# Two transformer layers on one core: GpSimd yields to VectorE's two-input operations, and the bias b2 moves to VectorE

## The chip, the cores and the metric

The kernel runs on one core of one Trainium2 chip. The metric is the device time of one execution in microseconds (us), as a median over runs. The core has five engines that each run their own instruction list in order and meet only at semaphores: TensorE (PE; PEld is its weight load), ScalarE (ACT), VectorE (DVE), GpSimd (POOL) and SyncE (SP), which issues the DMAs. Operands live in SBUF; TensorE writes to the eight banks of PSUM, 128 x 512 float32 each.

## The reference

Two layers with the same weights, each an attention block and a dense block, on 2048 tokens of width 512; 32 heads of width 16; the dense block is 1792 wide. All tensors are bf16.

```python
def _A_ref(x, wqkv, wo):
    qkv = (x @ wqkv).reshape(B, S, 3, H, Dh) ...
    scores = jnp.einsum("bhqd,bhkd->bhqk", q, k) * (Dh ** -0.5)
    p = _softmax(scores, axis=-1)
    o = jnp.einsum("bhqk,bhkd->bhqd", p, v)
    return o ... @ wo

def _B_ref(x, w1, b1, w2, b2):
    h = _gelu(jnp.einsum("bsd,df->bsf", x, w1) + b1)
    return jnp.einsum("bsf,fd->bsd", h, w2) + b2

x = x + _A_ref(_layernorm(x), A_wqkv, A_wo)
x = x + _B_ref(_layernorm(x), B_w1, B_b1, B_w2, B_b2)
# and the same two lines once more
```

## The kernel before

**Tiles and stages.** Tokens go in 16 tiles of 128, and queries in segments of 512 (the last segment of the second layer is split in two of 256). A layer is a long row of *passes*: a pass is one segment and four heads (for the two half segments, eight heads): 32 passes a layer, some of them cut in two by key range. A pass holds 64 *cells*: the scores of 128 keys against 512 query columns in one PSUM bank, their exponential, and the product of that with V, which adds up in PSUM bank 6. There are 4096 cells in all.

**Two ways for a cell.** Most cells go to ScalarE: `exps` (L1828) takes two or three banks in one exp instruction (L1846) and writes bf16 to a `pt` buffer. About 30% go by VectorE and GpSimd: `dfirst` (L1566) turns the scores into a 16-bit integer whose bits are an approximate power of two (L1568, tile `du`, or one of the lent tiles `kt` and `v`), and `dchain` (L1639) makes three shifted copies by two GpSimd integer additions (L1658 for one copy, L1662 for the two others), each of which is multiplied with a V scaled to it, so that the errors of the approximation average out. Those scaled copies of V, `vc`, are made by VectorE in `vcopies` (L1330).

**Around the passes.** VectorE also masks Q for each pass (`qpad`, L1347, tile `qp`), closes each pass (`norm`, L935: transpose out of bank 6, reciprocal, two-input product `ott` at L977, transpose to `otn`), adds the output projection to x (`wo`, L1014), normalises tiles (`ln`, L755, many small operations on `varr`, `rstd`, `ra`, `rb`, `nmr`, then `xln` at L802), adds b1 (L1123) and adds the dense block's result to x (`ytile`, L1174). The normalised tile goes through a DMA transpose to `xf` (L806, on SP's queue). TensorE does projections, dense layers (all recorded at L628, in groups of four 32-column matmuls side by side), scores (L1399) and P.V (L1912, with L1920 for the unused column groups).

**The order.** None of the engine lists is written by hand. Each piece of work is a generator that yields operations `_Op(engine, cost, ...)`; `_Sched` keeps a planned clock for each engine, takes from all threads the operation that can start first by that clock (ties by priority, a low number first), and appends it to its engine's list with the semaphore waits that its operands need. So the order on each engine is a result of the planned costs, and any change of a cost moves thousands of instructions. Every 24 us of planned ScalarE time, `tune` (L409) loads another of 15 sets of knobs, named by the list `PICKS` (L111).

**What the plan does about GpSimd and VectorE.** VectorE operations marked `port` (L239: those that write `ott`, `nmr`, `qp`, `vc`, `xln`, `varr`, `rstd`, `ra`, `rb` and a few more, reading first from SBUF) and GpSimd's additions are planned not to overlap. In `_ready` (L338) a GpSimd operation starts after the last `port` operation that began before it, and has an explicit wait for it; a `port` operation that would begin inside a planned GpSimd operation is planned at that operation's end. Priority does not enter there: a GpSimd addition that can start, starts.

**Filler.** Where a planned gap on TensorE is long enough and its density over the last 3.4 us (`WINDOW`) is under `WARM`, `fill` (L387) puts in matmuls whose result nobody reads (L1387).

**b2.** Row 0 of the tile `B2row` holds b2, the other rows are zeroed by GpSimd at the start (L646, L707). In `ytile` (L1148) the first operation of each tile begins with four matmuls of `ONES1` (ones in row 0) and `B2row` (L1167), which start the sum in PSUM; 14 further groups of four add the dense product, and L1174 adds the bank to x.

Of the kernel before, what the change touches and what calls it, by code (L numbers as in the profile page):

```python
# [5 lines left out]
ALU = mybir.AluOpType  # L6
# [8 lines left out]
D = 512  # L15
# [16 lines left out]
XT = 8  # L32
# [34 lines left out]
WTAIL = 2.8  # L67
RUSH = 8
# [42 lines left out]
PICKS = (1, 8, 1, 3, 1, 8, 1, 2, 8, 1, 8, 3, 0, 1, 1, 0, 0, 0, 0, 2, 1, 11, 8, 8,  # L111
         1, 8, 8, 3, 1, 1, 8, 1, 9, 8, 8, 1, 1, 8, 1, 3, 8, 1, 1, 8, 7, 2, 2, 14,
         7, 7, 1, 7, 7, 1, 9, 1, 1, 1, 1, 1)
# [115 lines left out]
class _Op:  # L229
    __slots__ = ("eng", "cost", "fns", "reads", "writes", "sem", "by", "tail", "prio", "mode", "slack", "late", "back", "port", "limit", "after")  # L230

    def __init__(self, eng, cost, fns, reads=(), writes=(), sem=None, by=1, tail=0.0, prio=None, mode="F", slack=None):
        self.eng, self.cost = eng, cost
        self.fns = fns if isinstance(fns, list) else [fns]
        self.reads, self.writes = list(reads), list(writes)
        self.sem, self.by, self.tail, self.prio, self.mode, self.slack = sem, by, tail, prio, mode, slack
        self.limit = 1e9
        self.late, self.after = None, []
        self.port = eng == "dve" and self.writes[:1] != [] and self.writes[0].startswith(("OTT", "NMR", "QP", "VC", "XLN", "PT", "V0", "V1", "VARR", "RSTD", "RA", "RB")) and not self.reads[:1] == [] and not self.reads[0].startswith("B.")  # L239
# [13 lines left out]
OWN = 0.022  # L253
HEAD = 0.14
LATENCY = {"pe": 0.219, "act": 0.21, "dve": 0.139, "pool": 0.153328, "sp": 0.1}
# [4 lines left out]
class _Sched:  # L260
# [77 lines left out]
    def _ready(self, op):  # L338
        t = 0.0
# [16 lines left out]
        return t  # L356

# [260 lines left out]
class _Plan:  # L618
# [12 lines left out]
    def init(self):  # L631
# [14 lines left out]
        yield _Op("pool", 0.3, lambda e: e.memset(T["B2row"][:], 0.0), writes=["B2zero"])  # L646
# [34 lines left out]
    def loads(self):  # L681
# [20 lines left out]
        for t in range(4, 8):  # L702
# [4 lines left out]
        yield _Op("sp", 0.2, lambda e: e.dma_start(T["B2row"][0:1, :], hbm["b2"].rearrange("(o e) -> o e", o=1)),  # L707
                  reads=["B2zero"], writes=["B2row", "B2zero"], sem="db2", by=16, tail=2.0)
# [46 lines left out]
    def ln(self, tiles, dst, dkeys, prio, quick=False, gate=()):  # L755
# [34 lines left out]
        for t in tiles:  # L790
            yield ("spawn", self.ln_tile(c, t, dst, dkeys, quick), prio)

    def ln_tile(self, c, t, dst, dkeys, quick):
# [5 lines left out]
        else:  # L799
# [348 lines left out]
    def ytile(self, l, seg, t):  # L1148
# [9 lines left out]
        for p in range(NFC // 2):  # L1158
# [11 lines left out]
            yield _Op("pe", len(fns) // 4 * MM, fns, reads=[wk, "ONES1", "B2row"] + ["G.%d.%d" % (f, t % 4) for f in (2 * p, 2 * p + 1)],  # L1170
                      writes=["B.%d" % b], prio=MID if p else FPRIO, mode="P")
# [149 lines left out]
    def vcopies(self):  # L1321
        T = self.T
        for l in range(NL):
            for j, kt in enumerate(KD[l]):
# [4 lines left out]
                for i, w in enumerate(VW):  # L1329
                    yield _Op("dve", 0.42, lambda e, j=j, i=i, w=w, src=src: e.tensor_scalar(  # L1330
# [5 lines left out]
    def qpad(self):  # L1336
        T = self.T
        for pi, (l, seg, g, kts, part, final) in enumerate(self.pas):
# [7 lines left out]
            for i, t in enumerate(ts):  # L1346
                yield _Op("dve", 0.15 + 0.262 * w / 512, lambda e, s=s, q=q, i=i, t=t, w=w: e.tensor_scalar(  # L1347
# [167 lines left out]
    def scores(self):  # L1515
        u = 0
        pools = self.s.pools
        while True:
# [24 lines left out]
            ahead = 0.065 + 0.4267 * self.held[1 - sl]  # L1543
# [284 lines left out]
    def exps(self):  # L1828
        T = self.T
        u = 0  # L1830
        while True:
# [14 lines left out]
            yield _Op("act", 0.065 + 0.4267 * n, lambda e, src=src, dst=dst: e.activation(  # L1846
# [178 lines left out]
```

## Time and profile before

Three runs took 1440.49, 1442.47 and 1443.03 us (median 1442.47). The profiled execution took 1441.41 us, of which its span, from the first to the last instruction, is 1439.5.

| | us, or as said | from |
|---|---|---|
| profiled execution / span | 1441.41 / 1439.5 | times, page |
| exps of two banks, `pt` alone | 893, mean 1.059 | ScalarE by form |
| exps of three banks, `pt` alone | 175, mean 1.503 | ScalarE by form |
| du, kt and v copies (L1568) | 1217, mean 0.68 | groups |
| GpSimd additions | 1240 in all, 0.60 and 1.02 for two cells | groups |
| filler matmuls, L1387 without the 13 at the start | 456 | PE by form |
| b2 matmuls | 128, mean 0.387 | PE by form |
| granted TensorE clock | 1.000 | cores |
| busy from 12 to 1411 us, of 1399.0 | PE 1357.2, ACT 1388.8, DVE 1195.7, POOL 1000.4 | windows |
| busy from 1411 us to the end, of 28.5 | PE 25.7, ACT 11.1, DVE 12.5, POOL 1.3 | windows |

A row of the groups reads: line, engine, operation, output<-input with shapes, count | busy us, mean ns of one | idle time of the engine just before such an instruction, and what ended most of it. Busy time counts overlapping instructions of an engine once, so an instruction's mean duration can be longer than the distance from its start to the next one's. A wait row reads: who waited, for whom: us in total, times, longest.

### The profile page before, as it was taken

What the parts mean: (1) busy time and instruction counts of PE and PEld (TensorE: products, weight loads), DVE (VectorE), ACT (ScalarE), POOL (GpSimd) and SP (SyncE); (2) the same over time, 40 slices, a digit from 0 to 9 for tenths busy, and PEclk for the clock granted to TensorE, in tenths of its full rate; (3) what the DMA queues carried; (4) which work ended last, traced back from release to release, by engine and by line L of the source; (5) the groups of instructions that cost most, each with busy time, mean ns of one, the idle gap of its engine ahead of it and who ended that gap; (6) DMA issues with size and microseconds to landing.
All of it is one profiled execution on the core that took longest, in us unless ns stands there. A gap on an engine that the chain in (4) does not pass through costs nothing.

```text
span 1439.5 us, 46034 instructions
## 1 busy us (share of the span) xinstructions
PE 1391.2 (97%) x19654; PEld 421.6 (29%) x19654; DVE 1215.7 (84%) x2266; ACT 1404.3 (98%) x1397; POOL 1006.0 (70%) x1261
## 2 busy tenths in 40 slices
PE   8999999999999999999999999999999999999998
PEld 3222222222222222222222222222222222344345
DVE  7789998978999889997988777999878986899774
ACT  7999999999999999999999999999999999999994
POOL 1177998767787686885757667658777876787670
PEclk9999999999999999999999999999999999999999
DMA  5200001153121531115321161100134115421443
GB/s 162 53 2 1 2 17 30 39 168 91 38 46 31 155 111 39 38 38 148 99 65 43 54 193 53 31 15 18 38 108 143 38 38 157 132 52 33 148 112 90
DMA packets 145047, 103.38 MB, mean 72 GB/s; under 512 B 37069, under 2 KB 143822, under 8 KB 144846
## 3 DMA queue, kind: packets, MB, share of 16 engines
q1 hardware_dynamic: 144846, 100.44, 24.5%
q8 instruction: 158, 2.59, 0.7%
q14 instruction: 43, 0.35, 0.1%
HBM read 88.61 MB, written 4.19 MB: 64 GB/s over the span
## 4 chain that ended last, share of the span: by engine, by line
ACT 47%; PE 36%; DVE 14%; DMA 2%; issue 1%; POOL 1%; SPq 0%; ACTq 0%
ACT pt L1846 36%; PE ps L628 12%; PE ps L1912 12%; PE ps L1399 11%; DVE du L1568 6%; ACT g L1144 3%; ACT v L1846 2%; ACT q L1846 2%; DVE kt L1568 2%; DMA xf<-xln 1%; ACT kt L1846 1%; ACT g L1846 1%; DVE v L1568 1%; DVE stats L762 1%; DVE xln L802 1%
## 5 line engine op out<-in xcount | busy, mean ns | idle before, releaser
L1846 ACT ACTIVATE pt<-ps 128x1024 bf16<-128x1024 f32 (+1 forms) x1069 | 1077.3, 1131 | 6.2 <-PE ps L1399 5.0
L1568 DVE TENSOR_SCALAR du<-ps 128x512 uint16<-128x512 f32 x899 | 597.6, 682 | 118.5 <-PE ps L1399 114.3
L1399 PE MATMUL ps<-qp,kt 32*128 32x512 bf16 x4096 | 535.0, 384 | 16.5 <-ACT pt L1846 9.2
L1662 POOL INT64_ADD du<-du x458 | 468.3, 1024 | 62.8 <-DVE qp L1347 9.4
L1658 POOL INT64_ADD du<-du x458 | 276.5, 605 | 248.1 <-DVE du L1568 194.5
L1912 PE MATMUL ps<-du,vc 128*17 128x512 bf16 (+1 forms) x3000 | 355.1, 359 | 3.5 <-POOL du L1662 1.1
L1399 PEld LDWEIGHTS ps<-qp,kt 32*128 32x128 bf16 x4096 | 137.8, 90 | 560.0 <-issue 175.6
L1912 PE MATMUL ps<-pt,v 128*17 128x512 bf16 (+1 forms) x2564 | 291.0, 360 | 4.4 <-ACT pt L1846 2.1
L1912 PE MATMUL ps<-du,v 128*17 128x512 bf16 (+1 forms) x1000 | 163.9, 360 | 5.7 <-issue 1.5
L628 PE MATMUL ps<-xf,wr 128*32 128x512 bf16 (+1 forms) x2272 | 160.7, 371 | 4.1 <-DMA xf<-xln 3.4
L1568 DVE TENSOR_SCALAR kt<-ps 128x512 uint16<-128x512 f32 x201 | 135.9, 684 | 26.7 <-PE ps L1399 25.2
L1912 PE MATMUL ps<-kt,vc 128*17 128x512 bf16 (+1 forms) x720 | 142.2, 346 | 0.7 <-POOL du L1662 0.4
L1912 PEld LDWEIGHTS ps<-du,vc 128*17 128x17 bf16 x3000 | 94.2, 89 | 81.4 <-issue 36.6
L1662 POOL INT64_ADD kt<-kt x103 | 104.9, 1019 | 12.3 <-DVE qp L1347 1.6
L628 PE MATMUL ps<-wr,g 128*32 128x512 bf16 x1504 | 110.9, 382 | 0.5 <-DMA wr<-in_B_w_dram 0.3
L1912 PEld LDWEIGHTS ps<-pt,v 128*17 128x17 bf16 x2564 | 69.2, 88 | 81.7 <-issue 51.0
L1123 DVE TENSOR_SCALAR g<-ps,hb1t 128x512 bf16<-128x512 f32 (+1 forms) x112 | 79.1, 708 | 13.6 <-PE ps L628 13.5
L1568 DVE TENSOR_SCALAR v<-ps 128x512 uint16<-128x512 f32 x117 | 79.1, 683 | 12.1 <-PE ps L1399 11.6
L1912 PE MATMUL ps<-kt,v 128*17 128x512 bf16 (+1 forms) x359 | 85.1, 358 | 3.0 <-DVE xt L968 1.3
L1658 POOL INT64_ADD kt<-kt x103 | 62.2, 604 | 34.5 <-DVE kt L1568 27.5
L1846 ACT ACTIVATE q<-ps 128x1024 bf16<-128x1024 f32 (+1 forms) x81 | 84.5, 1103 | 0.0
L1912 PE MATMUL ps<-v,vc 128*17 128x512 bf16 (+1 forms) x411 | 82.9, 350 | 0.6 <-DVE xln L802 0.5
(110 smaller groups left out, 1482.8 us busy)
## 6 DMA issues: line engine op xcount, KB each, us to landing
wr<-in_B_w_dram SPq DMA_DIRECT2D x243, 256.0 KB, 3.0
wr<-in_A_wqkv_dram SPq DMA_DIRECT2D x24, 256.0 KB, 2.9
wr<-in_A_wo_dram SPq DMA_DIRECT2D x17, 256.0 KB, 3.0
x<-in_A_x_dram SPq DMA_DIRECT2D x7, 512.0 KB, 4.1
pt<-in_B_w_dram SPq DMA_DIRECT2D x13, 256.0 KB, 3.7
kept<-x SPq DMA_DIRECT2D x4, 512.0 KB, 4.4
x<-kept SPq DMA_DIRECT2D x4, 512.0 KB, 4.0
out_dram<-x SPq DMA_DIRECT2D x16, 128.0 KB, 3.0
```

Source lines behind the costliest of these rows:

```text
L628: return [lambda e, a=a: e.matmul(out[32 * a:32 * a + 32, :], lhsT=lhsT[:, 32 * a:32 * a + 32], rhs=rhs, start=start, stop=stop, tile_posi ...
L762: yield _Op("dve", 0.66, lambda e, t=t: e.bn_stats(T["STATS"][:, t, :], T["X"][:, t % XT, :]), reads=["X.%d" % (t % XT)], writes=["ST.%d" ...
L802: yield _Op("dve", 0.41, lambda e: e.tensor_scalar(xl, T["X"][:, t % XT, :], T["RSTD"][:, t:t + 1], T["NMR"][:, t:t + 1], op0=ALU.mult, op ...
L1123: yield _Op("dve", 0.21 + n / 966, lambda e, fc=fc, pb=pb: e.tensor_scalar(T["G"][:, fc, q], pb, T["HB1T"][:, fc:fc + 1], None, op0=ALU.ad ...
L1144: lambda e, g=g: e.activation(out=g, in_=g, func=ACT.Gelu_apprx_tanh), reads=gk, writes=gk, prio=2)
L1399: return (lambda e: e.matmul(o, lhsT=lhsT, rhs=rhs, start=True, stop=True, tile_position=(32 * a, 0)), ["K%d.%d.%d" % (l, gb, kt // 4), "Q ...
L1568: yield _Op("dve", 0.682, lambda e: e.tensor_scalar(u, self.bank(b), E_SCALE, E_BIAS, op0=ALU.mult, op1=ALU.add), reads=["B.%d" % b], writ ...
L1658: yield _Op("pool", 0.151 + 0.2176 * n, lambda e: e.int64_add(words(1, 1), words(0, 1), SHIFT * ONES), reads=key[0], writes=key[1])
L1662: yield _Op("pool", 0.143 + 0.4352 * n, lambda e: e.int64_add(words(2, 2), words(0, 2), 2 * SHIFT * ONES), reads=key[0] + key[1], writes=k ...
L1846: yield _Op("act", 0.065 + 0.4267 * n, lambda e, src=src, dst=dst: e.activation(out=dst, in_=src, func=ACT.Exp, scale=0.25), reads=["B.%d" ...
L1912: op.fns.append(lambda e, o=o, lhsT=q[0][0][m], rhs=q[0][1][:, n * m:n * m + n], a=a, st=st, sp=sp: e.matmul(o, lhsT=lhsT, rhs=rhs, start= ...
```

## The change

Five edits, all in the planner's program:

1. **GpSimd yields.** A GpSimd operation is not a candidate while some thread's next operation is a `port` operation of priority 1 or lower number whose inputs are planned to be there within 0.6 us (`held_off`). Layer-norm threads have priority 0.2 or 0.3 (those of the first layer's opening 5 and up), `norm` threads 0.1 or 1, `qpad` and `vcopies` 4.
2. **b2 by VectorE.** `B2row` is loaded into all 128 rows by one DMA. As soon as a tile's `xln` is made for the dense block, a thread (priority of the norm plus 1) adds `B2row` to the tile's x in SBUF; `ytile` waits for it before its own sum. The four matmuls go, and the first dense matmul starts the sum in the bank. x is now also a `port` output when it is the b2 sum.
3. **Planned durations.** An exp costs 0.052 us plus 0.4267 a bank (was 0.065), a `qp` copy 0.08 + 0.262 (was 0.15 + 0.262), a `vc` copy 0.31 (was 0.42), and a DMA transpose lands 4.4 us after its issue (was 3.5).
4. **Another `PICKS`.**
5. GpSimd's memset of `B2row` goes.

```diff
+TTAIL = 4.4
-PICKS = (1, 8, 1, 3, 1, 8, 1, 2, 8, 1, 8, 3, 0, 1, 1, 0, 0, 0, 0, 2, 1, 11, 8, 8,
...
+PICKS = (1, 1, 2, 1, 2, 0, 1, 2, 1, 1, 11, 1, 2, 1, 2, 2, 1, 1, 2, 2, 2, 2, 1, 5,
...
-        self.port = eng == "dve" and ... "RSTD", "RA", "RB")) and ...
+        self.port = eng == "dve" and ... "RSTD", "RA", "RB", "X.")) and ...
+HOLDP = 1
+HOLDT = 0.6
         if op.eng == "pool":
+            if HOLDP and self.held_off(max(t, self.clock["pool"])):
+                return None
             t = max(t, self.last(max(t, self.clock["pool"]))[0])
+    def held_off(self, at):
+        for th in self.threads:
+            op = th.op
+            if op is not None and op.port and self._prio(op) <= HOLDP and all(k in self.P.lastw for k in op.reads):
+                t = max([self.end.get(ev, 0.0) - OWN * (ev[0] == "dve") for ev in self.P.deps(op.reads, op.writes)] + [0.0])
+                if t <= at + HOLDT:
+                    return True
+        return False
-        yield _Op("pool", 0.3, lambda e: e.memset(T["B2row"][:], 0.0), writes=["B2zero"])
-        yield _Op("sp", 0.2, lambda e: e.dma_start(T["B2row"][0:1, :], hbm["b2"].rearrange("(o e) -> o e", o=1)),
-                  reads=["B2zero"], writes=["B2row", "B2zero"], sem="db2", by=16, tail=2.0)
+        yield load(T["B2row"][:], hbm["b2"].rearrange("(o e) -> o e", o=1).to_broadcast([128, D]), "db2", ["B2row"], 0.4)
+    def bias(self, t, ph):
+        T = self.T
+        yield _Op("dve", 0.42, lambda e: e.tensor_tensor(out=T["X"][:, t % XT, :], in0=T["X"][:, t % XT, :], in1=T["B2row"][:, :], op=ALU.add),
+                  reads=["X.%d" % (t % XT), "B2row"], writes=["X.%d" % (t % XT)])
+        yield ("give", ("b2", ph // 2, t))
@@ ln_tile, behind xln @@
+        if ph % 2:
+            yield ("spawn", self.bias(t, ph), prio + 1)
-                      reads=["XLN.%d" % x], writes=dkeys(t), sem="dtr%d" % x, by=16, tail=3.5)
+                      reads=["XLN.%d" % x], writes=dkeys(t), sem="dtr%d" % x, by=16, tail=TTAIL)
@@ ytile @@
-            fns = [] if p else self.quads(pb, T["ONES1"][:, :], T["B2row"][:, :], True, False)
+            fns = []
             for j in range(2):
-                fns += self.quads(pb, T["G"][:, 2 * p + j, q], ws[j], False, p == last and j == 1)
+                fns += self.quads(pb, T["G"][:, 2 * p + j, q], ws[j], not (p or j), p == last and j == 1)
+        yield ("need", ("b2", l, t))
@@ vcopies, qpad, scores, exps @@
-                    yield _Op("dve", 0.42, ...
+                    yield _Op("dve", 0.31, ...
-                yield _Op("dve", 0.15 + 0.262 * w / 512, ...
+                yield _Op("dve", 0.08 + 0.262 * w / 512, ...
-            ahead = 0.065 + 0.4267 * self.held[1 - sl]
+            ahead = 0.052 + 0.4267 * self.held[1 - sl]
-            yield _Op("act", 0.065 + 0.4267 * n, ...
+            yield _Op("act", 0.052 + 0.4267 * n, ...
```

What the two planned programs hold, counted in their instruction lists:

| instructions | before | after |
|---|---|---|
| exps of three / two / one bank | 204 / 1133 / 1 | 177 / 1175 / 0 |
| score blocks copied by VectorE (L1568) | 1217 | 1215 |
| GpSimd additions | 1240 | 1232 |
| score matmuls, in so many unbroken runs | 4096, 1333 | 4096, 1356 |
| P.V matmuls with the zero ones beside them | 8984 | 8956 |
| filler matmuls without the 13 at the start | 456 | 320 |
| b2 matmuls / b2 additions on VectorE | 128 / 0 | 0 / 32 |
| explicit waits of GpSimd for VectorE | 710 | 718 |

More of the change, by code (lines that the diff above doesn't have):

```diff
@@ L238, in __init__ @@
         self.late, self.after = None, []
-        self.port = eng == "dve" and self.writes[:1] != [] and self.writes[0].startswith(("OTT", "NMR", "QP", "VC", "XLN", "PT", "V0", "V1", "VARR", "RSTD", "RA", "RB")) and not self.reads[:1] == [] and not self.reads[0].startswith("B.")
+        self.port = eng == "dve" and self.writes[:1] != [] and self.writes[0].startswith(("OTT", "NMR", "QP", "VC", "XLN", "PT", "V0", "V1", "VARR", "RSTD", "RA", "RB", "X.")) and not self.reads[:1] == [] and not self.reads[0].startswith("B.")
 class _Thread:
@@ L1166, in ytile @@
                 wk, ws = "WR.%d" % w, [T["WR"][w][:, 512 * j:512 * j + 512] for j in range(2)]
[L1167 removed]
+            fns = []
             for j in range(2):
[L1169 to L1170 removed]
+                fns += self.quads(pb, T["G"][:, 2 * p + j, q], ws[j], not (p or j), p == last and j == 1)
+            yield _Op("pe", len(fns) // 4 * MM, fns, reads=[wk] + ["G.%d.%d" % (f, t % 4) for f in (2 * p, 2 * p + 1)],
                       writes=["B.%d" % b], prio=MID if p else FPRIO, mode="P")
```

14 lines of the change are left out of this document (7 added, 7 removed).

## The prediction

> **What bounds the kernel now.** I read the page's busy shares and its chain first, then ScalarE by form, then the waits, then the places where ScalarE starts late. The page:
>
> ```profile
> PE 1391.2 (97%) x19654; PEld 421.6 (29%) x19654; DVE 1215.7 (84%) x2266; ACT 1404.3 (98%) x1397; POOL 1006.0 (70%) x1261
> ACT 47%; PE 36%; DVE 14%; DMA 2%; issue 1%; POOL 1%; SPq 0%; ACTq 0%
> ```
>
> ScalarE and TensorE are both full, and the chain hops between them: ScalarE cannot take an exp before TensorE has its scores, TensorE cannot write scores before ScalarE has freed the bank. VectorE and GpSimd have 224 and 433 us to spare. ScalarE by form, and a stretch of its timeline:
>
> ```profile
> L1846 ACT ACTIVATE pt<-ps 128x1024 bf16<-128x1024 f32 x893 | 856.1, 1059 | 5.4 <-PE ps L1399 4.3
> L1846 ACT ACTIVATE pt<-ps 128x1536 bf16<-128x1536 f32 x175 | 251.7, 1503 | 0.8 <-PE ps L1399 0.7
> ...
> 403.42 1.03 ACT L1846 ACTIVATE v<-ps 128x1024 bf16<-128x1024 f32 x1
> 404.32 7.91 ACT L1846 ACTIVATE pt<-ps 128x1024 bf16<-128x1024 f32 x8
> ```
>
> One two-bank exp lasts 1.03 to 1.06 us, but the next starts 0.90 us after it: exps overlap at their ends. Three banks go 1.33 us apart, so an exp costs 0.052 + 0.427 per bank. Summing start-to-start minus this price over the trace from 30 to 1404 us, ScalarE loses 36.1 us: 4 us in jitter under 0.03, 20.8 in 222 delays of 0.03 to 0.25, 11.3 in 24 longer ones. That is all an order can win back between the first and the last exp; 12 us of start and 28.5 of tail stand outside.
>
> **The change part by part**, against the profiled execution's 1441.41 us (span 1439.5 and 1.9 around it; the median of the runs, 1442.47, is 1.06 above it).
>
> *b2 off TensorE.* 32 tiles lose four matmuls each.
>
> ```profile
> 1430.02 0.39 PE L628 MATMUL ps<-b2row,ones 128*32 128x512 bf16 x4
> 1430.23 2.76 PE L628 MATMUL ps<-q,g 128*32 128x512 bf16 x48
> ```
>
> The four run side by side: what follows starts 0.21 us later, so 32 x 0.21 = 6.7 us. Four tiles lie after the last exp (1416.5, 1418.0, 1430.0, 1433.3), where TensorE works without a gap and sets the end: **-0.8**. The other 28 take 5.9 us out of the steady part.
>
> *The other order, on TensorE.* In the built programs' instruction order the 4096 score matmuls stand in 1356 runs instead of 1333. What a run costs:
>
> ```profile
> 1375.19 0.40 PE L1912 MATMUL ps<-du,v 128*17 128x256 bf16 x8
> 1375.41 0.39 PE L1912 MATMUL ps<-du,vc 128*17 128x256 bf16 x8
> 1375.73 0.39 PE L1399 MATMUL ps<-qp,kt 32*128 32x512 bf16 x3
> 1376.06 0.28 PE L1912 MATMUL ps<-v 128*17 128x256 bf16 x1
> ```
>
> Eight P.V matmuls take 0.22 (1375.19 to 1375.41); the score run starts 0.32 after the second eight, 0.10 more than that, and work behind it 0.33 later: 0.43 a run. 23 x 0.43 = +9.9; 28 fewer P.V and zero matmuls, four abreast, -1.5; b2 -5.9: +2.5 net. TensorE has 36% of the chain, so I count **+0.9** (ends: 0 and +2.5). 136 fewer filler matmuls (34 x 0.21 = 7.1 us) I take at nothing, since they are put where TensorE idles; were they in the way, 36% of it, -2.6, would be gained.
>
> *The other order, on ScalarE.* 1215 instead of 1217 score blocks go by VectorE and GpSimd, and 1352 exps instead of 1338: 2 x 0.427 + 14 x 0.052 = **+1.6**, all of it on the busiest engine (ends: +1.6 and, at the 47% share, +0.8).
>
> *GpSimd held back.* What it cures:
>
> ```profile
> L977 DVE TENSOR_TENSOR ott<-xt,rc 128x256 bf16<-128x256 f32 x56 | 36.1, 644 | 1.1
> L802 DVE TENSOR_SCALAR xln<-x,rstd,nmr 128x512 bf16<-128x512 bf16 x60 | 26.2, 469 | 2.9 <-DMA kt<-xln 2.0 <-DMA xf<-xln 0.7
> L780 DVE TENSOR_TENSOR ra<-rstd 128x4 f32<-128x4 f32 x20 | 5.0, 251 | 0.1
> ...
> L977 DVE TENSOR_TENSOR ott<-xt,rc x72: 277/424/1274, 92.0 to 1413.8; 128x256 bf16<-128x256 f32 x56, 128x128 bf16<-128x128 f32 x16
> ```
>
> The same ott lasts 0.42 or up to 1.27 us, as long as a GpSimd addition (1.02) more. By the records, 81 VectorE operations last over 0.12 us longer than the lower quartile of their kind, 33 us together; 62 of them (27 us: ott 13.9, the norm's small ones and xln 13.1) have a priority that the hold covers; the qp copies (5.3) do not. But VectorE has slack, and the price is what ScalarE feels: in the 5 us after those stalls it loses 10.7 us where its mean rate gives 8.1, in the 2 us after, 3.9 for 4.1. So **-1.5**, between 0 and 27 us x 14% of the chain = -3.8. One place:
>
> ```profile
> 523.03 1.04 POOL L1662 INT64_ADD du<-du  x1 [0.30 <-DVE rstd L783]
> 524.12 0.39 PE L1912 MATMUL ps<-du,v 128*17 128x512 bf16 x1 [0.41 <-POOL du L1662]
> ```
>
> The addition waited for the norm, P.V for the addition, and the exp after it came 0.56 late. The additions that are now begun later lie in GpSimd's 433 idle us; if that cover were gone, P.V would wait for them as here.
>
> *b2 added by VectorE.* 32 additions, two bf16 tiles in, one out. No row has it: nearest is xln (one tile in, 0.41 unhindered), then vc (0.29) and x<-x,ps (0.68, one input in PSUM). At 0.41: 13.1 us in VectorE's slack; 14% of that is 1.8, and most waits nowhere since the tile's own sum comes long after: **+0.5** (ends 0 and 0.68 x 32 x 14% = +3.0). The Trainium skill's page "VectorE: DVE Perf Modes" (Side-by-side: where the cycles go for N=2048 bf16) gives a two-input bf16 operation two elements a cycle behind some 158 cycles of start: an estimate of 0.43 us, which would leave the sum as it is. The memset that falls away (0.52 at the start on GpSimd) and the wider b2 load are both before anyone needs b2: nothing, at most the memset's 0.5.
>
> *Transposes planned 0.9 us later.* In the waits and at the worst place:
>
> ```profile
> PE ps L628 <- DMA xf<-xln: 3.4, 4, 1.3
> ...
> 880.88 0.61 PE L628 MATMUL ps<-xf,wr 128*32 128x512 bf16 x8 [1.28 <-DMA xf<-xln]
> 881.87 1.02 ACT L1846 ACTIVATE pt<-ps 128x1024 bf16<-128x1024 f32 x1 [1.08 <-PE ps L1399]
> ```
>
> TensorE's queue holds a projection whose input is not there; the scores stand behind it. Four such waits, and ScalarE starts 0.51, 0.91, 1.21 and 0.16 late behind them. With a later plan other work stands there: **-2.7** (ends 0 and -3.4).
>
> *The rest of the order.* 36.1 - 2.7 - 1.5 = 32 us of lateness remain, decided by where the planner puts each piece. Its new prices are nearer the trace: exp 0.052 + 0.427 a bank (it had 0.065), qp copy 0.342 (clean records 0.341, it had 0.412), vc 0.31 (0.29 clean, it had 0.42). By 36-us slices ScalarE loses 0.4 to 2.4 us, 0.8 in the middle one. Levelled to the middle one, 38 x 0.8 = 30: 6 less, of which the 4.2 above are part; to the best, 0.5: 17 less. Since a new order brings new late places too, I take **-4** (ends +6 and -13).
>
> Sum: -0.8 + 0.9 + 1.6 - 1.5 + 0.5 - 2.7 - 4 = -6.0: 1435.4 profiled, 1436.5 as a median.
>
> **Rivals.** *The order is worth more.* TensorE's fewer fillers mark fewer slack stretches; if all slices lose as little as the best, the rest gives -13 for -4: 1427.5. Against: 76 of the 136 fillers vanish in two of sixteen parts of the score sequence.
> *The stalls were hidden anyway.* ScalarE pays +1.6 and gets only the tail, -0.8, and half of the transposes, -1.4: 1442. For it: lateness after port stalls is no higher than elsewhere. This is also the time if the hold does not do what it says: it orders the plan's clock, and explicit GpSimd waits for VectorE rise only from 710 to 718.
> *The b2 addition collides.* Its priority is above the hold's bound, so GpSimd may have begun: ott's 28 stalls were 0.50 each. At 0.41 + 0.2 mean, it keeps the copies behind it from freeing PSUM banks for the scores. It decides where VectorE has under 0.6 us of slack behind it; at 24 of 32 places that is 14.6 us over a sum without its 0.5: 1450.5. Against: VectorE's copies waited 114 us for scores, so they usually have slack.
> *The clock drops.* Fewer fillers could let TensorE fall under the density that the kernel keeps over 3.4 us. Ten such windows at half speed cost 17 us: 1453. Against: the same rule places the fillers, the granted clock is 1.00 and the longest gap in the steady part 1.46 us. The page "TensorE: Matmul & The Clock Gate" of the Trainium skill (Part 1: The HAM clock gate) has the clock halve after an idle window of that length; no run here shows it.
>
> **How the numbers follow.** The forecast 0.55 (its own range 1430 to 1441), more from the order 0.13, hidden 0.17, colliding addition 0.13, clock 0.02. The likeliest gives **1436.5**. 1424 to 1448 leaves out part of the second, most of the fourth and the fifth, about 0.15. Within 0.2% (2.9 us, about what this measurement tells from no change) is 1439.6 to 1445.4: faster 0.50 + 0.13 + 0.01 = 0.64; same 0.05 + 0.14 = 0.19; slower 0.02 + 0.13 + 0.02 = 0.17.
>
> **What would show it.** ScalarE's lateness between first and last exp near 29 us; no wait of TensorE for xf<-xln over 0.3; ott's mean under 0.50 and the norm's small operations under 0.18; the b2 additions near 0.41; 1352 exps; a tail under 28 us. Wrong if ott falls and ScalarE's lateness stays at 36 (hidden), if rows of scores waiting for VectorE grow behind the b2 additions (colliding), or if score runs wait for GpSimd more than before.

## The result, and the profile after

The changed kernel takes 1449.82 us (median of 5 runs, 1449.70 to 1450.66) against 1443.03 for the kernel before in the same comparison: a ratio of 1.0050, 95% interval 1.0035 to 1.0065. The forecast was 1436.5, and 1449.8 lies above its range too. The profiled execution took 1449.72 us, its span is 1447.9. From the page of the changed kernel, the busy shares and the shares of the chain:

```profile
PE 1388.9 (96%) x19362; PEld 416.8 (29%) x19362; DVE 1233.6 (85%) x2296; ACT 1407.6 (97%) x1411; POOL 1002.4 (69%) x1252
ACT 44%; PE 32%; DVE 22%; POOL 2%; issue 1%; ACTq 0%; POOLq 0%; DVEq 0%
```

ScalarE and TensorE have as much to do as before. What moved is the chain: VectorE's share rises from 14 to 22%, though its busy time rose by only 18 us (1215.7 to 1233.6). ScalarE by form, and two rows of the waits:

```profile
L1867 ACT ACTIVATE pt<-ps 128x1024 bf16<-128x1024 f32 x899 | 863.8, 1081 | 10.9 <-PE ps L1420 9.4
L1867 ACT ACTIVATE pt<-ps 128x1536 bf16<-128x1536 f32 x155 | 225.5, 1521 | 2.9 <-PE ps L1420 2.6
...
PEld ps L1420 <- DVE du L1589: 95.2, 209, 1.0
ACT pt L1867 <- PE ps L1420: 12.0, 32, 1.0
```

The same two waits in the kernel before:

```profile
PEld ps L1399 <- DVE du L1568: 79.0, 188, 0.8
ACT pt L1846 <- PE ps L1399: 5.0, 10, 1.1
```

Score matmuls wait 16 us more for a VectorE copy (L1589, the old L1568) to free their bank, and exps wait 7 us more for scores. Read by the prediction's own measure, ScalarE's start-to-start minus 0.052 + 0.427 a bank, the lateness between first and last exp is 46.2 us, and 37.0 in the kernel before worked out the same way. The exps by that price come to 1.6 us more (two banks and 14 exps more), and together that puts the end of the last exp at 1421.8 instead of 1410.8. The tail behind it is 26.1 us instead of 28.7. So 11.0 lost before the last exp, 2.6 won after it: 8.4, the difference of the spans.

Where the lateness grew: I took, for each of 17 layer-norm chains, the time from its first `varr` to 3 us past its last `xln`. Inside these *norm stretches* lateness rose from 9.7 to 23.1 us; outside them it fell from 27.3 to 23.1. A chain from `varr` to `nmr` takes 5.57 us on average for 8.36 before, and 215 other VectorE instructions stand between `varr` and the last `xln` where there were 362. VectorE's rows by form show the rest:

```profile
L997 DVE TENSOR_TENSOR ott<-xt,rc 128x256 bf16<-128x256 f32 x56 | 33.2, 592 | 0.9
L820 DVE TENSOR_SCALAR xln<-x,rstd,nmr 128x512 bf16<-128x512 bf16 x60 | 27.5, 493 | 0.1
L807 DVE TENSOR_TENSOR x<-x,b2row 128x512 bf16<-128x512 bf16 x32 | 17.6, 563 | 0.0
L795 DVE SCALAR_TENSOR_TENSOR rstd<-rb,rstd 128x2 f32<-128x2 f32 x18 | 6.5, 362 | 0.4 <-DVE rb L793 0.2
L792 DVE TENSOR_TENSOR ra<-rstd 128x4 f32<-128x4 f32 x20 | 4.7, 234 | 0.1
```

The same `rstd` row in the kernel before:

```profile
L783 DVE SCALAR_TENSOR_TENSOR rstd<-rb,rstd 128x2 f32<-128x2 f32 x18 | 3.2, 177 | 0.2
```

The operations for which GpSimd is held back are not free of it. `ott` is a little shorter (644 to 592 ns), `xln` longer (469 to 493), and of the small operations some have grown, this `rstd` to twice its mean (177 to 362), and some have not (`ra` on 128x4, 251 to 234). In all, 105 VectorE operations last over 0.12 us longer than the lower quartile of their kind, 43.7 us together; before it was 81 and 33.2. One place, chosen rows of the timeline (start, duration, engine and instruction; idle time before it in brackets):

```profile
980.74 1.04 POOL L1683 INT64_ADD du<-du  x1 [0.17 <-DVE rstd L795]
981.11 0.69 DVE L792 TENSOR_TENSOR ra<-rstd 128x4 f32<-128x4 f32 x1
981.72 0.68 DVE L1589 TENSOR_SCALAR du<-ps 128x512 uint16<-128x512 f32 x1
982.32 0.14 DVE L793 SCALAR_TENSOR_TENSOR rb<-ra,varr 128x4 f32<-128x4 f32 x1
982.39 0.67 DVE L1589 TENSOR_SCALAR du<-ps 128x512 uint16<-128x512 f32 x1
982.45 0.39 PE L1420 MATMUL ps<-qp,kt 32*128 32x512 bf16 x3 [0.35 <-DVE du L1589]
983.12 0.38 PE L1420 MATMUL ps<-qp,kt 32*128 32x512 bf16 x1 [0.28 <-DVE du L1589]
...
984.28 1.94 ACT L1867 ACTIVATE pt<-ps 128x1024 bf16<-128x1024 f32 x2 [0.37 <-PE ps L1420]
984.57 0.39 PE L1420 MATMUL ps<-qp,kt 32*128 32x512 bf16 x3 [0.33 <-DVE du L1589]
985.03 1.50 DVE L820 TENSOR_SCALAR xln<-x,rstd,nmr 128x512 bf16<-128x512 bf16 x2
987.00 1.02 ACT L1867 ACTIVATE pt<-ps 128x1024 bf16<-128x1024 f32 x1 [0.78 <-PE ps L1420]
```

The addition starts at 980.74 and ends at 981.78. `ra`, four numbers a row, starts inside it and ends at 981.80: 0.69 us for an operation that takes 0.15 when nothing is in its way. The copy behind it frees its bank half a microsecond late, the scores behind the copies wait (0.35, 0.28, 0.33), and ScalarE stands idle for 0.37 and then 0.78 us. The Trainium skill, page "SBUF — State Buffer" (Who interferes with whom), says that VectorE shares one pair of SBUF ports with GpSimd, and that who issues first has it for its whole instruction while the other is blocked; these lines agree, `ra` ends 0.02 us behind the addition.

The 0.78 has a second cause besides. The windows of 3.4 us before and behind 985.40 (busy time of each engine, number of instructions in brackets, then the granted clock of TensorE):

```profile
core 0: us, PE busy (x) PEld busy (x) DVE busy (x) ACT busy (x) POOL busy (x), PEclk, DMA share, GB/s
981.99:985.40 3.41, 2.23 (x26) 0.61 (x26) 3.41 (x9) 3.04 (x4) 2.62 (x4) 1.00 0.01 2
985.40:988.82 3.42, 3.42 (x34) 0.55 (x26) 3.19 (x6) 2.15 (x3) 2.76 (x4) 0.50 0.21 42
```

While the scores waited, TensorE was busy 2.23 of 3.41 us, and for the next 3.4 us its clock was granted at half; there ScalarE lost 1.27 us, for 0.37 in the window before. This place alone, of all the norms in this trace, has that. It is not what makes the kernel slow: two of the five executions ran at a clock of 1.000 and took 1449.70 and 1449.97 us, as long as the others.

What lets that addition start there can be read in the code. While `ra` is a candidate, `held_off` keeps the addition out of the choice. As soon as `ra` has been placed, the addition is a candidate again. Its own start has not moved: it is the later of its inputs and GpSimd's clock, which lies up to 0.6 us *ahead* of `ra`. And `last` looks only at `port` operations that began at or before that start (`LEAN` is 0.0), so the addition gets neither a later start nor a wait. Going through the placed operations, in 84 of the 1232 additions a `port` operation is planned to begin inside the addition, over 0.2 us before its end (the addition itself begins 0.02 to 0.75 us ahead of that operation). In the kernel before this is so in none of the 1240, since such an operation is placed towards the addition's end. The hold thus removes the rule that kept room for the collision, and leaves the collision.

### The profile page after: what moved, and what is told of

Its sections match the earlier page's. It is cut to its first block, busy times and chain, and to the rows that moved or that the text cites. A ratio compares the mean times of both kernels' runs of the same rounds, so it can differ in the third digit from the quotient of the medians.

```text
span 1447.9 us, 45508 instructions
## 1 busy us (share of the span) xinstructions
PE 1388.9 (96%) x19362; PEld 416.8 (29%) x19362; DVE 1233.6 (85%) x2296; ACT 1407.6 (97%) x1411; POOL 1002.4 (69%) x1252
## 4 chain that ended last, share of the span: by engine, by line
ACT 44%; PE 32%; DVE 22%; POOL 2%; issue 1%; ACTq 0%; POOLq 0%; DVEq 0%
ACT pt L1867 31%; PE ps L1420 10%; PE ps L1933 10%; PE ps L642 10%; DVE du L1589 8%; ACT q L1867 3%; ACT v L1867 3%; ACT g L1164 3%; DVE kt L1589 2%; ACT kt L1867 2%; POOL du L1683 1%; DVE xln L820 1%; DVE v L1589 1%; DVE ott L997 1%; DVE stats L774 1%
## 5 line engine op out<-in xcount | busy, mean ns | idle before, releaser
L1867 ACT ACTIVATE pt<-ps 128x1024 bf16<-128x1024 f32 (+1 forms) x1054 | 1060.1, 1146 | 13.8 <-PE ps L1420 12.0
L1589 DVE TENSOR_SCALAR du<-ps 128x512 uint16<-128x512 f32 x896 | 598.7, 683 | 110.5 <-PE ps L1420 105.2
L1420 PE MATMUL ps<-qp,kt 32*128 32x512 bf16 x4096 | 540.1, 384 | 27.3 <-ACT pt L1867 10.0
L1933 PE MATMUL ps<-du,vc 128*17 128x512 bf16 (+1 forms) x2988 | 347.3, 360 | 4.5 <-POOL du L1683 1.2
L1420 PEld LDWEIGHTS ps<-qp,kt 32*128 32x128 bf16 x4096 | 141.6, 91 | 582.9 <-issue 184.3
L1933 PE MATMUL ps<-pt,v 128*17 128x512 bf16 (+1 forms) x2523 | 283.4, 359 | 4.2 <-ACT pt L1867 2.2
L1589 DVE TENSOR_SCALAR kt<-ps 128x512 uint16<-128x512 f32 x201 | 134.9, 682 | 25.8 <-PE ps L1420 25.1
L1933 PE MATMUL ps<-kt,vc 128*17 128x512 bf16 (+1 forms) x723 | 133.8, 345 | 1.4 <-DVE du L1589 0.5
L1933 PEld LDWEIGHTS ps<-du,vc 128*17 128x17 bf16 x2988 | 92.2, 89 | 82.4 <-issue 36.2
L1589 DVE TENSOR_SCALAR v<-ps 128x512 uint16<-128x512 f32 x118 | 79.3, 683 | 14.8 <-PE ps L1420 14.7
L1867 ACT ACTIVATE q<-ps 128x1024 bf16<-128x1024 f32 (+1 forms) x83 | 88.1, 1132 | 0.6 <-PE ps L1420 0.5
L1867 ACT ACTIVATE g<-ps 128x1024 bf16<-128x1024 f32 (+1 forms) x85 | 84.8, 1116 | 0.8 <-PE ps L1420 0.5
```

What stands on the lines that cost most here:

```text
L1420: return (lambda e: e.matmul(o, lhsT=lhsT, rhs=rhs, start=True, stop=True, tile_position=(32 * a, 0)), ["K%d.%d.%d" % (l, gb, kt // 4), "Q ...
L1589: yield _Op("dve", 0.682, lambda e: e.tensor_scalar(u, self.bank(b), E_SCALE, E_BIAS, op0=ALU.mult, op1=ALU.add), reads=["B.%d" % b], writ ...
L1867: yield _Op("act", 0.052 + 0.4267 * n, lambda e, src=src, dst=dst: e.activation(out=dst, in_=src, func=ACT.Exp, scale=0.25), reads=["B.%d" ...
L1933: op.fns.append(lambda e, o=o, lhsT=q[0][0][m], rhs=q[0][1][:, n * m:n * m + n], a=a, st=st, sp=sp: e.matmul(o, lhsT=lhsT, rhs=rhs, start= ...
```

## The experiments

Each run is compared with the kernel before on the same chip. Ratios carry their 95% intervals; where they are turned into time, 0.001 is 1.44 us. "Stalls" and "lateness" are measured as above.

| run | median us | ratio (interval) | stalls: number, us | lateness us |
|---|---|---|---|---|
| changed kernel | 1449.82 | 1.0050 (1.0035 to 1.0065) | 105, 43.7 | 46.2 |
| e1, hold off | 1452.05 | 1.0077 (1.0060 to 1.0093) | 92, 37.8 | 32.7 |
| e2, hold alone | 1471.48 | 1.0210 (1.0195 to 1.0225) | 96, 42.4 | 64.1 |
| e3, b2 sum on 2 columns | 1446.85 | 1.0042 (1.0027 to 1.0057) | 96, 40.8 | 42.9 |
| e4, all additions short | 1425.79 | 0.9893 (0.9878 to 0.9908) | 5, 0.9 | 20.9 |
| e5, forgotten waits added | 1449.47 | 1.0054 (1.0039 to 1.0069) | 88, 36.2 | 46.2 |
| e6, the same on e2 | 1461.94 | 1.0139 (1.0124 to 1.0154) | 63, 26.7 | 51.2 |
| e7, before, all additions short | 1432.70 | 0.9936 (0.9920 to 0.9953) | 4, 0.8 | 27.4 |
| e8, P.V does not wait for GpSimd | 1447.49 | 1.0040 (1.0025 to 1.0055) | 110, 46.2 | 42.9 |
| e9, 84 held additions short | 1427.83 | 0.9897 (0.9877 to 0.9916) | 39, 11.0 | 23.0 |
| e10, 84 others short | 1447.71 | 1.0039 (1.0027 to 1.0051) | 88, 38.9 | 43.3 |
| e11, hold made good, choices anew | 1439.09 | 0.9981 (0.9972 to 0.9990) | 61, 23.0 | 29.7 |
| e12, hold off, choices anew | 1438.89 | 0.9975 (0.9966 to 0.9985) | 87, 33.9 | 25.9 |
| e13, as e11, other choices | 1439.40 | 0.9989 (0.9979 to 0.9998) | 59, 20.4 | 27.9 |
| e14, as e12, other choices | 1443.12 | 1.0010 (1.0001 to 1.0019) | 88, 35.2 | 27.1 |
| e15, 65 held additions at norms short | 1428.60 | 0.9907 (0.9894 to 0.9921) | 62, 20.7 | 24.8 |
| e16, the other 19 short | 1447.35 | 1.0040 (1.0026 to 1.0053) | 85, 35.0 | 43.2 |

### The hold alone, and all but the hold

```diff
 # e1, on the changed kernel
-HOLDP = 1
+HOLDP = 0
 # e2, on the kernel before
+HOLDP = 1
+HOLDT = 0.6
         if op.eng == "pool":
+            if HOLDP and self.held_off(max(t, self.clock["pool"])):
+                return None
```

> The changed kernel without the hold on GpSimd (planned anew, so the order moves; 28 more score blocks go by ScalarE, 1351 exps: 11.9 us more ScalarE work than the changed kernel). Packing theory (the hold packs the layer norm's operations on VectorE, the copies of scores that free PSUM banks wait behind them, the next scores and then ScalarE are late): ScalarE's lateness in the stretches from varr to 3 us past the last xln falls from 23 to about 10 us, in all from 46 to about 33, time 1449.8 + 11.9 - 13 = 1449. Rival, the b2 addition or the order in general is the cause: lateness stays near 46, time 1460 or more.

> The kernel before with the hold alone (planned anew; 9 more score blocks by ScalarE, 1347 exps: 4.3 us more work than before). Packing theory: lateness in the norm stretches rises from 10 to about 20 us, time 1443 + 4.3 + 10 = 1457. Rival (b2 or the other prices are the cause): only the work, 1447.

e2 is 30 us slower than the kernel before: the hold by itself does harm, in an order that was found without it. The harm is twice what its expectation had, 1457. Its norm stretches show the same signs as the changed kernel's, chains of 5.58 us and 25.0 us of lateness (16 chains), and its plan has 105 additions with a `port` operation inside them as counted above. Part of the 30 us is TensorE's clock: it was 0.992 to 0.995 in all four executions, and the trace has 20.5 us at half clock, in four places that begin in a norm stretch or within 5 us behind one.

e1 takes 13.5 us of lateness off the changed kernel, as expected, and its plan has no such addition. But it gives the time back: the replanned order sends 28 fewer blocks by VectorE and GpSimd (1187 for 1215), which is 11.9 us more of priced exps, and its tail is 29.8 us for 26.1. It fits that the lateness goes with the hold, but doesn't show what the hold costs in time: switching a rule off in a planner with choices tuned to it is not the removal of one cost. e1's order also leaves part of the second layer's first 512 queries changed.

### The b2 sum narrowed, GpSimd taken away

```diff
 # e3
-out=T["X"][:, t % XT, :], in0=T["X"][:, t % XT, :], in1=T["B2row"][:, :], op=ALU.add),
+out=T["X"][:, t % XT, 0:2], in0=T["X"][:, t % XT, 0:2], in1=T["B2row"][:, 0:2], op=ALU.add),
 # e4, and e7 on the kernel before
-e.int64_add(words(1, 1), words(0, 1), SHIFT * ONES)
+e.int64_add(words(1, 1)[:, 0:8], words(0, 1)[:, 0:8], SHIFT * ONES)
...
-(ws, T["DU"][du][:, i, jj, :].bitcast(BF16), wk + ["DU.%d.%d.%d" % (du, i, jj)],
+(ws, T["DU"][du][:, 0, jj, :].bitcast(BF16), wk + ["DU.%d.%d.%d" % (du, i, jj), "DU.%d.0.%d" % (du, jj)],
```

> The changed kernel, same order on every engine, with the b2 addition on 2 of 512 columns (most of b2 is left out). Packing theory: 32 x (0.56 - 0.15) = 13 us come off VectorE, but outside the place that decides: 0 to 2 us less, 1448 to 1450. Rival, the b2 addition collides and sets the loss: 5 us or more less, 1445 or below.

> The changed kernel, same order on every engine, with GpSimd's additions on 8 of 512 or more words, and P.V reading the first copy in place of the other three (the softmax approximation's averaging is left out). If VectorE's stalls against GpSimd (44 us in 105 operations) make the packed norm late: stalls gone, lateness in the norm stretches falls from 23 to under 12, time 1438 or below. If the packing alone does it, without stalls: lateness there stays above 18, and only the 4 us behind late GpSimd additions go, 1445 to 1447.

> The kernel before, same order, with GpSimd's additions on 8 words and P.V reading the first copy (the averaging is left out): the control to the same edit in the changed kernel (1425.8). If the change loses by collisions with GpSimd, before gains less from the edit than after's 24 us: 1425 to 1432, so that the two differ by under 4 us or after is ahead. If the loss lies in packing or order, before stays 7 us ahead: about 1419.

These keep each kernel's order, so they are clean. Narrowing the b2 sum gives 1.2 us by the ratios and 3.0 by the medians: some 1 to 3 us is what b2's sum on VectorE costs, and as the intervals overlap it can't be told from nothing. The second edit of e4 and e7 shortens the other addition of each chain in the same way; TensorE's products still wait for both additions but read the chain's first slot (the copy itself instead of its shifts), which is the part left changed. Without GpSimd in the way the changed kernel is 6.2 us *faster* than the kernel before (0.9893 against 0.9936; by the intervals 3 to 9); e7 itself ends just above its expected 1425 to 1432. So the other parts of the change are a gain, and what turns it round is what GpSimd's additions cost: 9.2 us in the kernel before (1 - 0.9936), 22.6 in the changed one (1.0050 - 0.9893). The b2 rows of e4:

```profile
L807 DVE TENSOR_TENSOR x<-x,b2row 128x512 bf16<-128x512 bf16 x32 | 12.7, 410 | 0.0
L792 DVE TENSOR_TENSOR ra<-rstd 128x4 f32<-128x4 f32 x20 | 3.0, 152 | 0.1
```

Unhindered, the b2 sum takes 0.410 us and `ra` 0.152.

### Does TensorE wait for additions that come late, and is it only the forgotten wait?

```diff
 # e8: the first slot is read, and
-            if sem == "pe" and eng == "pe":
+            if sem == "pe" and eng == "pe" or sem == "pool" and eng == "pe" and val > 20:
                 continue
 # e5 on the changed kernel, e6 on e2
-    def last(self, at):
+    def last(self, at, lean=LEAN0):
...
-                over = self.last(start)[1]
+                over = self.last(start, HOLDT)[1]
```

> The changed kernel, same order, GpSimd's additions whole, but P.V reads the first copy and does not wait for GpSimd (the averaging is left out). It takes away late additions as a cause and leaves the collisions. Theory 'hold forgets': 4 us behind late additions go, 1444 to 1447. Rival, additions that come late for P.V are the loss: 1440 or below.

> The changed kernel, same order on every engine; each GpSimd addition also waits for the last two-input VectorE operation that the planner had placed up to 0.6 us behind its planned start, which the hold skipped over and forgot. Theory 'hold forgets' (held additions are placed at their old time, inside the operation that they were held for, without a wait, win the port on the chip and stall VectorE): VectorE's stalls fall from 105 (44 us) to under 40 (12 us), lateness in the norm stretches from 23 to about 14, some of it comes back as P.V waiting for later additions; time 1437 to 1444. Rival, packing without collisions: stalls fall but lateness and time stay, 1448 or more.

> The same added wait in the kernel before with the hold alone (order as in that run, 1471.5). Theory 'hold forgets': stalls fall from 96 to under 40 and the time by 10 us or more, below 1461. Rival, packing or this run's order: 1467 or more.

e8 leaves every addition at work and takes away TensorE's wait for it: 1.4 us. In exchange its products read the first slot, and VectorE, which had known of the additions through TensorE, has 576 explicit waits for them. Additions that come late for P.V are not the loss; the rival in which the hold simply delays GpSimd falls. e5 puts in the waits that the plan forgot, in the same order: nothing. That is the time its rival named, packing without collisions. But the collisions are not gone, 88 stalls for 105 where under 40 were expected, so the run doesn't test that rival (e4 does: in the same packed order, without stalls, the time falls by 22.6 us). The stalls moved: those of `ott` fell from 10.9 to 7.2 us, those of the b2 sum and of `ra` rose from 8.1 to 11.6. In the order of e2 the same edit takes the stalls from 96 to 63 (under 40 was expected) and gives 10 us; part of that is the clock, since executions of the two at 0.994 lie some 6 us apart (1469.5 and 1463.5). So this alone does not settle the cause.

### The same order, few additions short

```diff
+SHORT = {151, 152, 153, 155, 156, 162, 163, 232, 233, 235, 237, 255, ...}
+def short(w, done=False):
+    k = ADDS[0]
+    ADDS[0] += done
+    if k not in SHORT:
+        return w
+    return w[:, 0:8] if len(w.shape) == 2 else w[:, :, 0:8]
-e.int64_add(words(1, 1), words(0, 1), SHIFT * ONES)
+e.int64_add(short(words(1, 1)), short(words(0, 1), True), SHIFT * ONES)
```

> The changed kernel's exact order of instructions. 84 of its 1232 GpSimd additions, those that the planner lets begin over 0.2 us before a layer-norm or softmax operation of VectorE that then falls inside them, add 8 words instead of the whole slot (so these numerators are left wrong); the other 1148 are whole. All additions short gave 1425.8 against the changed kernel's 1449.8: 24 us. Theory (the collisions that the hold lets through, and what they make late, are most of what was lost): 1432 to 1439, VectorE stalls from 105 to below 40. Rival (every addition costs a little, by its share of the 1232; the held ones are not special): 1448, 24 x 84/1232 = 1.6 us faster.

> The control to the run before: the same order, and as many additions short, 84, drawn at random from those that the planner has begin with no such operation inside them. Theory: 1446.5 to 1449, stalls of VectorE within 10 of the changed kernel's 105. Rival (it's the amount of GpSimd work, about 84 x 0.8 us, that counts, wherever it lies): the same gain as in the run before.

As in e4, the second addition has the same edit and all these products read the first slot. The 84 held additions, 7% of 1232, carry 22 us of what GpSimd costs (1.0050 - 0.9897 = 0.0153); 84 others, as many and nearly as long (67 us in the changed kernel for 74), 1.6 us. That is more than the theory asked for, and the amount of GpSimd work is out as a cause. The control lost 17 stalls with that, more than was expected, and hardly any time. The next two split the 84.

> The changed kernel's exact order, short (8 words, these numerators wrong, and the weighted sums read the first slot in all pairs, as in e4, e9 and e10) only in those 65 of the 84 held additions in which a layer norm's operation was placed. Theory (the loss is in the norms' chains, each small operation of which waits for a whole addition, while copies queue behind): 1430 to 1435. Rival (the loss goes with the number of held additions, 22 x 65/84 = 17 us): the two can't be told apart by this run alone, but with the next: 17 against 5; the theory has 18 to 20 against 2 to 4.

> The same with the other 19 of the 84, those with a softmax operation inside them (a division's product or a masked query). Theory: 1444 to 1446, that is 2 to 4 us below e10's 1447.7, which stands for the reading of the first slot and 84 others short. Rival (the share by number): 22 x 19/84 = 5 us below 1449.8, 1443.

The 65 at layer norms carry 20.6 us, the 19 at softmax operations 1.4, no more than the control and less than the 2 to 4 below it that was expected. VectorE's rows in e15, then in e16:

```profile
L1009 DVE TENSOR_TENSOR ott<-xt,rc 128x256 bf16<-128x256 f32 x56 | 33.4, 597 | 0.9
L832 DVE TENSOR_SCALAR xln<-x,rstd,nmr 128x512 bf16<-128x512 bf16 x60 | 21.8, 400 | 0.1
```

```profile
L1009 DVE TENSOR_TENSOR ott<-xt,rc 128x256 bf16<-128x256 f32 x56 | 27.8, 496 | 0.9
L832 DVE TENSOR_SCALAR xln<-x,rstd,nmr 128x512 bf16<-128x512 bf16 x60 | 27.3, 490 | 0.1
```

e16 takes 8.7 us of stall off VectorE (43.7 to 35.0), mostly off `ott`, and the time hardly moves; e15 takes 23.0 off and the time falls by 20.6. A stalled microsecond in a layer norm costs almost a microsecond, and one at `ott` nothing that shows. The windows tell why. The stretch of the timeline above, from the copy at 979.78 to the end of `xln`, in the changed kernel and then the same place in e15 (columns as in the windows above):

```profile
979.78:986.53 6.75, 5.35 (x54) 1.23 (x51) 6.75 (x16) 5.80 (x6) 4.99 (x7) 0.92 0.00 1
```

```profile
965.97:971.29 5.32, 4.62 (x55) 1.40 (x55) 5.32 (x17) 5.32 (x7) 2.46 (x6) 1.00 0.00 2
```

The third of the engines, VectorE, is busy for the whole stretch in both, 6.75 of 6.75 and 5.32 of 5.32. There is no slack for a stall to vanish in: without four of the additions the same work is over 1.43 us sooner, and ScalarE, the fourth, which lost 0.95 us there, loses none. (The clock of 0.92 in the first line is the last 1.1 us, at half; 0.64 of the 0.95 us were lost before that, and in e15 the clock stays at 1.00.) Chosen rows of e15's timeline at the same place:

```profile
965.58 7.43 ACT L1879 ACTIVATE pt<-ps 128x1024 bf16<-128x1024 f32 x8
966.81 0.21 POOL L1695 INT64_ADD du<-du  x1 [0.47 <-DVE rstd L807]
967.24 0.15 DVE L804 TENSOR_TENSOR ra<-rstd 128x4 f32<-128x4 f32 x1
967.31 0.68 DVE L1601 TENSOR_SCALAR du<-ps 128x512 uint16<-128x512 f32 x1
...
970.57 0.72 DVE L832 TENSOR_SCALAR xln<-x,rstd,nmr 128x512 bf16<-128x512 bf16 x2
```

`ra` takes 0.15 for 0.69, the two `xln` 0.72 for 1.50, and eight exps follow each other unbroken. The tight chain by itself is not the harm: in e15, the same order, it is tighter still (4.46 us for 5.57).

### The hold made good, and the hold off, each with its own choices

```diff
 # e11, e13
-LEAN = 0.0
+LEAN = 0.6
 # e12, e14
-HOLDP = 1
+HOLDP = 0
 # all four
-PICKS = (1, 1, 2, 1, 2, 0, 1, 2, 1, 1, 11, 1, 2, 1, 2, 2, 1, 1, 2, 2, 2, 2, 1, 5,
...
+PICKS = (1, 7, 1, 1, 1, 10, 1, 2, 1, 10, 4, 13, 8, 10, 14, 1, 7, 0, 7, 13, 2, 10, 1, 5, ...
```

> The changed kernel with the hold made good: an addition that comes out within 0.6 us ahead of a layer-norm or softmax operation of VectorE already placed is placed behind it, with a wait on it; and the 60 choices of the order searched anew for that rule. Everything is computed. Theory (the held additions that start all the same are the loss, the rest of the change is worth some 6 us): 1432 to 1440, VectorE stalls below 60, the norm stretches less late than the 23 us of the changed kernel. Rival (holding GpSimd off by itself costs more than the collisions, as additions then come late for TensorE): 1445 or more.

> The changed kernel with the hold off and the 60 choices of the order searched anew without it; b2 by VectorE, the transposes' due time and the other times kept. Everything is computed. In the first such run the choices were those found with the hold, and 12 us of ScalarE work came in with 1351 instead of 1395 exponentials' length. Theory (without the hold the rest of the change gains, as the prediction's terms had it, 1 to 8 us): 1434 to 1441. Rival (the hold is not to blame; b2 by VectorE and the other order lose by themselves): above 1445.

> As e11: the changed kernel with the hold made good (an addition that comes out within 0.6 us ahead of a placed layer-norm or softmax operation goes behind it, with a wait), and with another set of the 60 choices of the order, one that computes all four heads of the second layer's first 512 rows that e11's order changes. Theory (the rest of the change is worth some 3 to 6 us once the held additions stay out): 1436 to 1441, as e11's 1439.1, VectorE stalls 50 to 75. Rival (e11's time was due to what it leaves changed): 1443 or more.

> As e12: the changed kernel with the hold off, and with another set of the 60 choices that computes all that e12's order changes. Theory (a hold that is made good and no hold at all come out alike, since GpSimd has no idle time to give away without TensorE waiting for its additions): 1438 to 1443, within 3 us of e13. Rival (the hold, once made good, is worth what the prediction's upper end gave it, 3.8 us): e13 is 3 us or more below this run.

Contrary to what their expectations say, e11 and e12 do not compute everything: like e1 they leave part of the second layer's first 512 queries changed. They are evidence on the time of such an order and not versions to use; e13 and e14 compute all. With `LEAN` at 0.6 an addition that would start up to 0.6 us ahead of a placed `port` operation goes behind it; in e13's plan 7 of the additions are left with a `port` operation inside them, in e14's, without the hold, none. VectorE's rows in e13:

```profile
L995 DVE TENSOR_TENSOR ott<-xt,rc 128x256 bf16<-128x256 f32 x56 | 26.8, 478 | 1.2
L818 DVE TENSOR_SCALAR xln<-x,rstd,nmr 128x512 bf16<-128x512 bf16 x60 | 24.2, 438 | 2.0 <-DMA kt<-xln 1.8
L793 DVE SCALAR_TENSOR_TENSOR rstd<-rb,rstd 128x2 f32<-128x2 f32 x18 | 3.2, 177 | 0.2
L790 DVE TENSOR_TENSOR ra<-rstd 128x4 f32<-128x4 f32 x20 | 3.7, 187 | 0.1
```

Against the changed kernel's 592, 493, 362 and 234 these are what the prediction wanted to see, with 59 stalls of 20.4 us and 7.1 us of lateness in the norm stretches instead of 23.1. e13 takes 8.8 us off the changed kernel (1.0050 to 0.9989) and lies just under the kernel before; its exps cost 7.7 us more than those of before by the price (17 banks and 9 exps more), which eats most of the 9.1 us that it gains in lateness. e13 and e14 are 3.0 us apart by their ratios and 3.7 by the medians, which meets the rival's condition that a hold made good is worth some 3 us. Since the two have different choices for the order, that is not shown to be the hold's doing, and e12, which has no hold, was as fast as e11. What the four share is that every one is at least 5.8 us below the changed kernel.

## Why the prediction was wrong

**The step that failed: "GpSimd held back".** The sum gave it -1.5, "between 0 and 27 us x 14% of the chain = -3.8". Measured as the difference of what the additions cost in the two orders, it is +22.6 - 9.2 = +13.4 us; the orders differ in other choices too, but 22 of the 22.6 us lie in the 84 additions, and the kernel before has none of that kind. Two assumptions fell. The first is that held additions "are now begun later" and lie in GpSimd's idle time. 84 of them begin before the operation that they were held for. The prediction had the sign of this in hand: the hold "orders the plan's clock", and explicit waits for VectorE rise only from 710 to 718. It priced that as a hold without effect, 1442, and did not go on to ask what the plan does with an operation that it believes free: it draws up the norm's chain without room (8.36 to 5.57 us), with fewer copies between. The second is the price. It bounded what a stall is worth by 14%, VectorE's share of the chain over the whole span, with 0 as the worst. e15 and e16 show two prices: 20.6 us for 23.0 us of stall at the norms, 1.4 for 8.7 elsewhere, mostly at `ott`. An average over stages hid a stage in which VectorE is full. (A small misreading stands beside it: the longest `ott` is 0.85 us above the usual one, 1.27 for 0.42, and not 1.02.)

**b2.** Right in kind. TensorE's b2 matmuls left the tail and it became 2.6 us shorter, where -0.8 was forecast for them alone; the runs do not say how much of the 2.6 is b2. It need not be any: e1 and e14 have no b2 matmuls either, and tails of 29.8 and 30.1. On VectorE the sum takes 0.410 us unhindered, as taken from `xln`'s 0.41, but 0.563 among GpSimd's additions, and it costs 1 to 3 us (e3) for the +0.5, inside its ends of 0 and +3.0. The rival that had it collide is true as to the collision (0.15 us each for the 0.2 assumed), and far too dear: 1 to 3 us and not 14.6. In how many of its 32 places VectorE is full was not counted.

**ScalarE's order** stands at +1.6: the trace has the 1352 exps, and the last exp ends 11.0 us later, 9.2 of it lateness. **TensorE's order** was not measured by itself.

**Transposes.** No wait of TensorE for xf<-xln is left in the waits, from 3.4 us: the step did what it says. **The rest of the order**, the transposes among it, was -6.7 together. Lateness outside the norm stretches fell by 4.2, and with GpSimd out of both kernels the changed one is 6.2 us faster (e4 against e7) where the sum without the hold's term is -4.5. As a sum these terms stand; how the 6.2 divides among them no run shows. -4.5 + 13.4 = +8.9 in place of -6.0 is the whole error of the sum, to within 2 us of the +7.2 that the ratio gives.

**The signs that it named.** Lateness near 29: 46.2. `ott` under 0.50: 0.592. The norm's small operations under 0.18: 0.15 to 0.49 by row. The b2 additions near 0.41: 0.563. A tail under 28: 26.1. "Rows of scores waiting for VectorE" did grow, as the prediction said of the case in which it is wrong, but behind the norm's operations more than behind the b2 sum: the 95.2 us of waits for `du` copies become 80.9 in e15 and 91.0 in e3. P.V waits for GpSimd's `du` a little more than before (36.7 us for 32.8); taking all such waits away gave 1.4 us (e8). The clock did halve for 3.4 us in the profiled execution, in a norm, and its mean stayed at 0.999; the rival in which it costs 17 us did not come. (The window "of that length" in that rival is its 3.4 us, not the gap of 1.46.)

## What to carry to other kernels

A rule that keeps work back while something else is due has to say where that work goes once the other is placed; if its own start time stays, it lands just ahead of what it was kept from, and a planner that believes the place is free can make it worse than no rule, as e2 was. To price a stall, look at the stalled engine in the few microseconds around it, not at its share of the span: where it was busy 100%, 20.6 of 23.0 stalled us were lost here, and elsewhere next to none of 8.7. To find out which of many overlaps cost time, keep the order and shorten only those, beside as many others.

## What was not expected of the hardware

A GpSimd addition costs far more by where it starts than by what it does: 65 additions, 5% of them, carry 20.6 us, and 84 others of nearly the same length 1.6. An operation on 128x4 numbers can be stalled as long as a whole addition has left to run: `ra` took 0.69 us for its 0.15 and ended 0.02 us after the addition did. And a wait added to keep an addition out of one operation moved the collision to the next (e5: 105 stalls to 88, the time unchanged), and VectorE's full stretches leave few gaps to start it in; that this is why was argued and not tried. Last, TensorE's clock went to half for 3.4 us right behind a window of that length in which TensorE was busy 2.23 us and never idle for over 0.35 us at a time; in e15, busy 2.71 us at the same place, it stayed full.
